# Identity matrices built on chip, a smaller load of constants, and a stored order in place of a planned one

## The chip, the cores and the metric

The kernel runs on one core of one Trainium2 chip. The metric is the time of one execution in microseconds of the device (us), the median of several executions. The engines are PE (TensorE, matmuls), DVE (VectorE), ACT (ScalarE), POOL (GpSimd) and SP (SyncE, which here only issues DMAs).

## What is computed

The inputs are q, k and v of shape (4, 8, 768, 64): 4 batches, 8 heads, 768 positions, 64 features. Attention is limited by a hash, and its result goes through a two-layer network:

```
q_bits = (q @ proj > 0); k_bits = (k @ proj > 0)        # proj is 64 x 6
mask   = bucket(q_bits) == bucket(k_bits)                # 6 bits make a bucket number
scores = where(mask, q @ k.T / 8, -1e9)
attn   = softmax(scores); x = (attn @ v) as (3072, 512)
h      = max(x @ w_in, 0)                                # w_in is 512 x 2048
out    = (h * h) @ w_out                                 # w_out is 2048 x 512
```

## The kernel before

**The work.** The program goes through 48 visits, one for each batch, third of the positions and pair of heads. A visit has four units of 128 queries (two heads, two blocks each). In a unit PE makes 128x768 scores in PSUM (`pS`, or `side`, or a bank of `po`), DVE takes the row maximum (tile `line`), ACT takes the exponential (tile `e`) with the row sums, and the reciprocal of the sums is `rv`. The masks need no work of their own: the keys and queries are extended by 64 rows that hold the codes of their buckets, so that one matmul adds a large negative number where the buckets differ.

**The preparation of a pair of heads** (`prep`) has these steps: the load of keys and queries (`A` and `Q` in the first batch, `R` later); the projection matmuls `pd`, which write `side` from `A`, `Q` and the projection `pj`; their signs `bits` by ACT; two matmuls per head with the code matrix `sgn` (`pc`, also in `side`); and DVE and ACT, which turn these into the extra rows. In the first batch, visits run "plain", in float32: the attention is transposed by PE against the identity `unit_f` (`pT`). Later visits use pairs of float16 numbers and transpose by DMA. The values V of a batch are scaled by their largest column norm, for which `dg` is made from a second identity, `ident` (`scale_values`).

**The network.** When the four pairs of heads of a third are done, its 256 rows go through both layers (`moe`): matmuls `pm` with `win`, ReLU and square, then matmuls `po` with `wo`. The weights are read, unpacked and split into two float16 parts during the first visits (`split_win`, `split_wout`, in the buffer `room`).

**The constants** (lines 806 to 833). `pj` (12 KB) and `cst` are loaded from ACT's DMA queue; `cst` is a tile of 128 rows whose first four columns are mask constants and whose other 128 columns are codes, of which rows 0 to 31 are used. `unit_f`, a 128x128 float32 identity, is loaded from SP's queue, and DVE copies it to `ident` in bfloat16 (line 832). In the planned program `cst` goes out ahead of `pj`. `bounded` (line 931) rescales two columns of `cst` by a factor tile `fac` once, before the first pair of heads that isn't plain.

**The order.** All operations are first written down in a list (`Program.add`) with the engines that may do each and the buffers they touch. `order` (line 509) then decides which engine does each operation, and in which order each engine has them, by a list scheduler (`forward`, `backward`) with a model of durations (`cost`, `LAGS`), shaken by about 1,500 stored seeds (`PATH`). The orders are fixed when the program is built: each engine takes its instructions strictly in turn, so one that waits holds back all behind it on its engine. In the model a small load from memory lands 2.2 us after its issue, whatever is queued in front of it (line 578). `emit` also puts matmuls of no use (`idle<-ones`) where the model sees PE idle before the first transposes.

Of the kernel before, what the change touches and what calls it, by code (L numbers as in the profile page):

```python
# [45 lines left out]
PRICE = dict(pe=1, dve=3.57, act=0.3, pool=3.06, sp=0.43)  # L46

EARLY, EARLY_TO = dict(pe=1, dve=1.5, act=1, pool=1, sp=0.43), 150000
AHEAD, DELAY, LAG = 60, 2500, 1.0

ROUNDS, BEHIND = 24, 40000
PATH = (
# [1253 lines left out]
```

## Time and profile before

| what | value |
|---|---|
| median of 3 executions | 869.58 us (869.0 to 869.71) |
| profiled execution: span from the first to the last instruction | 865.2 us |
| time around the span: median less span | 4.4 us |
| PE busy | 835.6 us (97%) |
| DVE busy | 660.7 us (76%) |
| ACT busy | 673.4 us (78%) |
| POOL busy | 73.7 us (9%) |
| HBM read | 37.36 MB |
| mean granted clock of TensorE | 0.994 of 2.4 GHz |

The page gives the profiled execution's span alone and no time around it; the 4.4 us are the median less that span. Busy shares are means over a span whose parts have different limits, so the stretches at the start are looked at by themselves below. A matmul in float32 leaves two records where one in float16 leaves one.

### The profile page before, as it was taken

What the parts mean: (1) busy time and instruction counts of PE and PEld (TensorE: products, weight loads), DVE (VectorE), ACT (ScalarE), POOL (GpSimd) and SP (SyncE); (2) the same over time, 40 slices, a digit from 0 to 9 for tenths busy, and PEclk for the clock granted to TensorE, in tenths of its full rate; (3) what the DMA queues carried; (4) which work ended last, traced back from release to release, by engine and by line L of the source; (5) the groups of instructions that cost most, each with busy time, mean ns of one, the idle gap of its engine ahead of it and who ended that gap; (6) DMA issues with size and microseconds to landing.
All of it is one profiled execution on the core that took longest, in us unless ns stands there. A gap on an engine that the chain in (4) does not pass through costs nothing. (4 is left out here: it accounts for less than half of the span.)

```text
span 865.2 us, 17070 instructions
## 1 busy us (share of the span) xinstructions
PE 835.6 (97%) x6386; PEld 548.4 (63%) x6386; DVE 660.7 (76%) x1450; ACT 673.4 (78%) x1185; POOL 73.7 (9%) x156
## 2 busy tenths in 40 slices
PE   6899899998999999999999999999999999999997
...
PEclk8999999999999999999999999999999999999999
...
GB/s 317 70 124 191 182 183 195 190 144 82 145 189 177 184 131 167 154 161 178 156 155 165 149 156 146 168 160 108 156 155 111 145 149 157 122 93 80 1 25 25
DMA packets 295361, 124.19 MB, mean 144 GB/s; under 512 B 273520, under 2 KB 281456, under 8 KB 295280
## 3 DMA queue, kind: packets, MB, share of 16 engines
...
HBM read 37.36 MB, written 6.29 MB: 50 GB/s over the span
## 5 line engine op out<-in xcount | busy, mean ns | idle before, releaser
L746 PE MATMUL pm<-xx,win 128*128 128x256 f16 x2304 | 308.7, 273 | 1.0 <-ACT g L746 0.7
L746 PE MATMUL po<-wo,g 128*128 128x512 f16 x1152 | 303.1, 379 | 5.1 <-ACT acc L746 2.9
L746 PEld LDWEIGHTS <-win 128*128 128x128 f16 x2304 | 223.4, 98 | 80.4 <-issue 12.8
L746 DVE SCALAR_TENSOR_TENSOR hl<-e,rv,hl 128x768 f16<-128x768 f32 x172 | 173.2, 1015 | 18.6 <-ACT hl L746 16.4
L746 PEld LDWEIGHTS <-g 128*128 128x128 f16 x1152 | 111.5, 98 | 104.5 <-issue 14.6
L746 ACT ACTIVATE hl<-e,rv 128x768 f16<-128x768 f32 x161 | 147.6, 928 | 8.6 <-DMA aT<-hl 7.5
L746 DVE SCALAR_TENSOR_TENSOR g<-g,g 128x512 f16<-128x512 f32 x90 | 61.8, 687 | 80.3 <-ACT g L746 80.0
L746 ACT ACTIVATE g<-g 128x512 f32<-128x512 f32 (+1 forms) x183 | 113.7, 626 | 8.9 <-PE po L746 6.5
L744 DVE TENSOR_REDUCE line<-pS 128x1 f32<-128x768 f32 x113 | 107.5, 952 | 14.1 <-PE pS L746 13.2
L746 ACT ACTIVATE g<-pm 128x512 f32<-128x512 f32 x94 | 55.5, 590 | 69.2 <-PE pm L746 66.7
L739 PE MATMUL pA<-aT,VV 128*64 128x256 f16 x1548 | 92.7, 274 | 0.0
L739 PEld LDWEIGHTS <-VV 128*64 128x64 f16 x1548 | 81.2, 110 | 14.2 <-issue 13.9
L746 ACT ACTIVATE e<-pS,pair 128x768 f32<-128x768 f32 x72 | 70.8, 984 | 17.8 <-DVE pair L744 12.6
L746 ACT ACTIVATE e<-side,pair 128x768 f32<-128x768 f32 x72 | 71.0, 987 | 14.6 <-DVE pair L744 9.7
L746 POOL TENSOR_SCALAR rv<-sm 128x1 f32<-128x1 f32 x104 | 32.7, 314 | 581.3 <-ACT e L746 579.4
L744 DVE TENSOR_REDUCE line<-side 128x1 f32<-128x768 f32 x79 | 75.2, 952 | 5.9 <-PE side L746 5.6
L746 ACT ACTIVATE e<-pS,line 128x768 f32<-128x768 f32 x41 | 36.8, 897 | 11.4 <-DVE line L744 10.1
L746 PEld LDWEIGHTS <-room 128*128 128x128 f16 x288 | 27.6, 98 | 19.0 <-issue 2.1
L746 PE MATMUL pS<-A,L 128*128 128x384 f32 x84 | 32.3, 494 | 2.2 <-ACT e L746 1.3
L746 PE MATMUL side<-room 128*128 128x384 f16 x144 | 34.3, 326 | 0.0
L746 PE MATMUL pS<-room 128*128 128x384 f16 x144 | 33.7, 326 | 0.4 <-ACT e L746 0.3
L746 PE MATMUL pS<-Q,M 128*128 128x384 f32 x80 | 32.2, 512 | 0.9 <-ACT e L746 0.6
...
## 6 DMA issues: line engine op xcount, KB each, us to landing
...
```

Of the source, the lines that this page charges most:

```text
L739: ins = q.engine.matmul(*map(real, args), **kw).ins
L744: issue(q, getattr(q.engine, name)(*map(real, args), **{k: real(x) for k, x in kw.items()}).ins)
L746: ins = getattr(q.engine, o.name)(*map(real, o.args), **{k: real(x) for k, x in o.kw.items()}).ins
```

## The change

The identities `unit_f` and `ident` are no longer loaded and copied: two `affine_select` instructions on POOL keep the diagonal of the tile of ones. Of the codes only rows 0 to 31 are loaded (16 KB in place of 66 KB). The mask constants become four memsets on POOL, at the size that `bounded` used to make with `fac`. The order in which the batch's first values are loaded is changed (`SPLITS`). The scheduler and its seeds are gone: a table packed into text (`ORDER`) holds the place of each operation and the engine that does it. The model stays only to place the idle matmuls; in it a small load now lands after 2.9 us (`LANDS`). The place where the idle matmuls stop is found as the first operation, in the new order, that uses their PSUM buffer.

```diff
+SPLITS = (1, 3, 0, 2)
...
-TRANSPOSES, HBM, SMALL = 165, 265, 300
+TRANSPOSES, HBM, SMALL, LANDS = 165, 265, 300, 2900
...
     def order(self):
         self.prepare()
-        out = self.rounds()
-        prio = None
-        for seed in PATH:
...
+        table = np.frombuffer(zlib.decompress(base64.b85decode("".join(ORDER.split()))), np.uint8).reshape(3, len(self.ops)).astype(int)
+        left = list(range(len(self.ops)))
+        out = [left.pop(n) for n in table[0] + 256 * table[1]]
+        for o, way in zip(self.ops, table[2]):
+            o.queue, o.name, o.args, o.kw = o.ways[way][:4]
+        self.replay(out)
         return out
...
                 if o.ways[0][4][1] < SMALL:
-                    dma, done = at0, busy + 2200
+                    dma, done = at0, busy + LANDS
...
-        for i in out[: out.index(self.busy_from)]:
+        busy = set().union(*(rec.ops for rec in self.idle[0].rec.line))
+        for i in out:
             o = self.ops[i]
+            if i in busy:
+                break
...
     act.dma_start(pj[:, 0 : 4 * NB], proj2[:, NB : 5 * NB])
-    both_f = sb([P, 4 + P], F32, "cst")
-    cst = both_f[:, 0:4]
-    act.dma_start(both_f, consts[:, 0 : 4 + P])
+    codes = sb([32, P], F32, "codes")
+    act.dma_start(codes, consts[0:32, 4 : 4 + P])
...
-        move(sgn[32 * n : 32 * n + 32, n * P : (n + 1) * P], both_f[0:32, 4:], 1.0, (dve, pool) if n else (dve,))
+        move(sgn[32 * n : 32 * n + 32, n * P : (n + 1) * P], codes, 1.0, (dve, pool) if n else (dve,))
...
-    unit_f = sb([P, P], F32, "unit_f")
-    sp.dma_start(unit_f, consts[:, 4 + 2 * P :])
-    ident = sb([P, P], BF16, "ident")
-    dve.tensor_copy(ident, unit_f)
+    unit_f, ident = sb([P, P], F32, "unit_f"), sb([P, P], BF16, "ident")
+    for x in (unit_f, ident):
+        pool.affine_select(x, ones, pattern=[[-1, P]], compare_op=ALU.is_equal, fill=0.0, base=0, channel_multiplier=1)
+    cst = sb([P, 2], F32, "cst")
+    for h, x, least in ((T, NB / 2 * MASK, -MASK), (U, (NB / 2 - 1) * MASK, 0.0)):
+        pool.memset(cst[h, 0:1], x)
+        pool.memset(cst[h, 1:2], least)
...
     def bounded(Rs):
         if not halved:
-            fac = sb([P, 1], F32, "fac")
-            for h, x in ((T, MASK / BIG), (U, MASK)):
-                dve.memset(fac[h], x)
-            dve.tensor_scalar(cst[:, 0:2], cst[:, 0:2], fac, 1.0, ALU.mult, ALU.mult)
...
-        for hp in range(H // 2) if b else START[1]:
+        for hp in range(H // 2) if b else SPLITS:
```

## Rows read from the trace of the kernel before

**Rows 1.** The page, 40 slices of 21.6 us: busy tenths, and PE's clock

```profile
PE   6899899998999999999999999999999999999997
PEclk8999999999999999999999999999999999999999
```

**Rows 2.** Busy us (instructions) by stretch: PE, weight load, DVE, ACT, POOL, clock, DMA

```profile
12.00:16.00 4.00, 0.78 (x3) 0.26 (x2) 0.03 (x1) 0.00 (x0) 0.00 (x0) 1.00 1.04 412
16.00:18.00 2.00, 0.30 (x1) 0.00 (x0) 1.94 (x4) 0.90 (x2) 0.00 (x0) 0.50 1.00 402
18.00:24.00 6.00, 6.00 (x23) 3.21 (x23) 4.27 (x10) 4.35 (x11) 2.86 (x4) 0.60 0.63 184
24.00:35.00 11.00, 8.70 (x50) 4.96 (x50) 10.33 (x29) 10.50 (x27) 1.15 (x2) 1.00 0.12 36
35.00:50.00 15.00, 13.53 (x84) 7.31 (x80) 13.51 (x27) 11.44 (x27) 2.92 (x7) 1.00 0.35 106
50.00:100.00 50.00, 45.42 (x274) 27.08 (x275) 45.96 (x103) 46.20 (x95) 18.75 (x31) 1.00 0.69 174
100.00:300.00 200.00, 194.64 (x1393) 124.44 (x1392) 173.81 (x378) 169.56 (x290) 26.81 (x45) 1.00 0.74 163
300.00:600.00 300.00, 297.56 (x2481) 199.72 (x2479) 245.85 (x542) 251.12 (x437) 12.77 (x42) 1.00 0.81 157
600.00:850.00 250.00, 248.59 (x1947) 167.98 (x1945) 157.44 (x340) 170.93 (x292) 7.67 (x20) 1.00 0.55 103
```

**Rows 3.** Timeline of the stall: start, us, engine, line, operation [idle before <-releaser]

```profile
8.92 0.33 SPq L746 DMA_DIRECT2D unit_f<-consts  x1
9.77 2.20 PE L746 MATMUL pS<-A,L 128*128 128x384 f32 x6 [0.94 <-ACT L L746]
...
15.97 0.23 DVE L746 CAST ident<-unit_f 128x128 bf16<-128x128 f32 x1 [6.35 <-DMA unit_f<-consts]
16.12 0.95 DVE L744 TENSOR_REDUCE line<-pS 128x1 f32<-128x768 f32 x1
...
18.14 1.54 PE L746 MATMUL pT<-unit_f,e 128*128 128x128 f32 x6
```

**Rows 4.** Waits in 0 to 35 us: who <- whom: us, times, longest

```profile
DVE ident L746 <- DMA unit_f<-consts: 6.3, 1, 6.3
...
ACT bits L746 <- PE pS L746: 1.5, 1, 1.5
...
DVE line L744 <- PE pS L746: 0.5, 1, 0.5
```

**Rows 5.** Timeline of the first loads and their users

```profile
0.73 0.41 ACTq L746 DMA_DIRECT2D cst<-consts  x1
...
1.17 0.46 ACTq L746 DMA_DIRECT2D pj<-proj  x1
1.19 0.42 SPq L746 DMA_DIRECT2D Q<-kq  x1
...
4.93 0.29 POOL L746 TENSOR_SCALAR sgn<-cst 32x128 bf16<-32x128 f32 x1 [3.91 <-DMA cst<-consts]
...
5.93 0.14 PEld L739 LDWEIGHTS side<-A,pj 128*32 128x32 f32 x3
```

**Rows 6.** Tiles `pj`, `Q` (0 to 20 us), `unit_f`, in turn: issue to landing

```profile
DMA to landing us min/median/max: 4.7/4.7/4.7
...
DMA to landing us min/median/max: 4.4/5.5/8.1
...
DMA to landing us min/median/max: 7.0/7.0/7.0
```

**Rows 7.** Groups of instructions on POOL: count | busy us, mean ns | idle before

```profile
L746 POOL TENSOR_TENSOR g<-g,g 128x512 f16<-128x512 f32 x6 | 7.6, 1260 | 33.9 <-ACT g L746 31.4 <-DVE g L746 2.4
...
L746 POOL TENSOR_SCALAR dg<-ident,top 128x128 bf16<-128x128 bf16 x1 | 0.4, 372 | 7.5 <-DVE top L746 7.5
```

**Rows 8.** Busy us in one stretch of 25 us

```profile
200.00:225.00 25.00, 22.39 (x178) 13.45 (x175) 20.01 (x46) 19.95 (x28) 0.19 (x1) 1.00 0.63 128
```

More of the change, by code (lines that the diff above doesn't have):

```diff
@@ L1 @@
-import heapq
-import random
+import base64
+import zlib
 from contextlib import ExitStack
@@ L45 @@
 BUFS = dict(xx=16, hl=3, e=3, aT=3, g=2, A=3, Q=3, L=3, M=3, RV=2, VV=6)
[L46 to L52, printed above, removed]
[194 rows of a table removed]
-)
+LAG = 1.0
+ORDER = """
+c-rlH2Vhji*8e#(x9x7WZ?f5JHY5-OBq5DR=*>pxT|`6>siBH=5KxK;$X}!=JVd2E0Z~8{1q2_8C{jd40>~o}nt)QJ!#8txH+%0UDEOhDzW+O6Z`-*uXU_c2IlnUt6(EYBj1m|vqDfXjY$b}K&~(s{
+4(1Mk(4PI_=FKp<*(4zB{sE9BR|g5~AYj|_@CXsw2!f%lC^`j_*0>swMzo0~nGjD!h&Dl)G$IjKX+aP~;`0(}ChRhDv?vI6A<C%;f+Xb#tfvU0jD|E2p|Y5l3_uBFBD96l6@=ChUkOT;L--^Pe7;zv
@@ new lines @@
+dwjCDRDr0JtqVSSvlcB=gEkNn9<JdLqL-ATWr5W7W=FOMPl5};l4`Ly!Qn8cO^C8XspN<VM??#6M3OBTY;Kz=&SZ+nF%gJ1Sd0dPp+c1>U4|zNk;cc%RkRvvwoNiXT0~``wA=x*vD6GD3DWO@#Ml({
+lF2c(v&z<tNs2*_r*bl_OQWOR_qf~D5ZqOx9!5whmE!`Z%jHT02h?jB1sV1@yVKs#Zma1@hIsbHeKwobnq8kAZB-%izBI5nvKyqBt2@jtu;xH2_5qTdMKZ-IAYlbxybohrW=LMIS7;0#8eKLz`XP_U
+BM9zNG}7a#?ukLy1FT!9Sh-dfW;-$*4&q9C$K|ry9f;OUYhvlFjD#e##APS=(qb*I`YOhF(-GV$QShFpK?M_(a~T25WhEjfnxrxy3M&{2L?ZMSgzJJ(P7s`eDscMJ>0f^OnNoU&(&Gv}dZG%GT!|k3
+85$fobqH%a3$nA1X48sXFe}TRnVFfNX~%RXjx>x)$j7bU`w*Nl<x*42?MV5k9Q>>H7D(D~akCK;%a)as-oY={FZ+0tEHA|+ON{abpKt9VpU*J=)cpBzanc)J?>m+0oH=ss*_CEh+Ea1Wd^%H@F=J;Y
@@ new lines @@
+OoJt4>eQ)=(r6AzO`QZOui=CV6R>>w)bi8Eu6%V&%5&3~v9%dBDr2O1;bij&bCTI?E?sWm$XNpijvB$P`<uB;HV-gIv$M-=hKTOH9j=}>=z>o|CxcaL+Y##4t&6SdRIO8|PU|{#8Ur?y<tFHnCEB<i
+b=MbZo%<eoAiEZ&4_430qM6m$?C;IwV*4Z$a?&c<($cII%4b%{sF0Bnm6e@sP08Y7EtN?!BFm?zv+vW=%xO@;>cS+m-5Qac%>E_YY-R99X<9llv2<B1edV4Dm#-Tykt<YbCNyn&x+#;NPs&ZWD2*F8
+{-tqaQqZVTBe~(8h7HRL_1)j)=ZZUbMbWK->+AbnTed~gFI-=`;}JGGVn2i2jk&p|Tqa=iIH}VKmMBY%<((^*8)<O$;@e9vxT{n-pIX_L<CoWRa*pQA&aqXhR0$$1d-ol1{M(Xgx4@pXTD5l8s#VKc
+vnJGl>V|4xLRBsslqyELmcKb9CnpBr^OdAxMfWFJ26(%3=2}YMLehyzhc};qj`&)K4mNZ+9H(cxXTD~gZne6mx~$d~Et*;LC)&ZbyD>Df+9Kfv>u3TKM;c(n_>9rQsEMPVeIAAylxGxWv@)PZ4XJwd
@@ new lines @@
+0VDh4h(Y~DsV@g;mACp=sWPl*_q;)*SLLpiJN4_{xpP<O`D9<A2XuP+3EGA9Z4X@@%gPgk$MF$F6oj@y3t5&O&5g~I*uAB>0U<ZHMXt}(q`r4W?t@+cc!+(VX02+qYu2#UAQ5)Ey)x5Lv}ReEqzV=$
+<;q(8Vm3#V@_{K9j4_f&bVs@UVs*PQDk@5jjFciJ7v(<eWOCIB(j@^d+Q>DA|I0q#4RSj6eC$uLzu-yXTnraDES)?moHz<cP8~Z@c=*Wa!opKWqR*Z<3{XH$5>hDdKkE2lpW~3jQQ+9U=j47z{sG5c
+$6;n%7QD9uY=c-~>(*UczZBrh%~Vn(=~LH6Hu?sq)3|m6Yv%aa;V`Z;n$2s>?{m*s#y-p0XDRm#C<WkKXmG>4IV>&UKaiPX#w?f#Cdh>8Mq}E`Mx&7!;f3or6K+go;ngtS@C!c~oTChepA3eR2E&hr
+i}G=L@)$i!jgsMz;oy~n5d{Y~9N18}YX9kog7;3r$^&ci^H;*ZfkOT}s{nSevED@s{u3c?Q{0z?EFxs_k`0R&Z&(|%e8t>(i+t}dUF!3#I8A1gISUCPhuLQu`@BisV8<zh%kwZ}CIY47rqXAhl~iG;
@@ new lines @@
+anjJqV}`P;XUC83CJpL3P?81?dw%42X#hMb_7layuk(l~_7|B7UGQmqs+%A@A&RkivFPQ}-s^4S^|n;6*+nz2w=cA*-<mCyC%2)ea~pR9to0B#RaL=Rr}2Xi)NRPty-rkA_4`?9?I~B50V;vz$&9Qu
+S(T1wt+r$bfU_UU&V%H#0LC&#<7}gnV2Cp$#3_nbiB%MIqlA$__-ff4)MAe@+w5k$$!K?gjSI0_(Rx$5af1@`HNJ@aaFsAbpE-jH3TK7W;u-uA(RR{yTz!LOMw_j`i3cPUL6CQWl)vlS?<D36vIILg
+aIV6o%a`HeSG%^rxy=Bl0e*t3r#8X~I0fgw5SV2P3ne&s&}b|;z(DW=uti@1?<zkitG?Z}>^+6ax0G&?7IF9aCv1c_mMpyri$7jGe+_>EtJ&uR8D=e9uwvoc3xI3=&zH<IAtEB;%{L+@vQxzDh%FKL
+0^+lDD*cp>nKnflIZm1)jgW@%)iezT;}8*`A4q)-L;DRGVCYK*C`0px%o;kxWa@4*nR=O2>1l%Y2v79t-7c?Vk7ro)=%y$glz=p4i`BCI<Kkm2+5yyW0ni#G5XHF-AN)sy*$R2^mHSmVvsN{*S}heE
@@ new lines @@
+%wSA1g{;)!X&GrlMy3vaMi?X{3+2_^*)Os0puv3y4io@HQc4iyuCm+%Jn%Rnd5;qoe;)19`EjJolUkEj@M!B!Pj>1Atw{6MgaEXaX~QNB8@Fso+dLvRYt^7-{U&0YN1BPPTl+_DDvI^QfK(Q%iPhDs
+x;eG)6*Fo8+zUYkQ-u^Esd7$|aPPfBd8DN&7vz2sOGp%>YocU{wK;4MZG%`#Y>dSN)Dh*2jqp;*W0hn@wy0i2MWocA207sOH?I@*%;h>EXU~#zYOmyHxN_z)$QNZ93@0vKI`-qmBNq<Axx$l$hkv<n
+;YVYE@nC`R*eOLJ1;?2&3r?IoaiSnT9|~B6IRvl^ASER=e@A)v9=?Wvd<kCoT)p}ngbj>cg5X&1SieRwn^#A`hism!&15wLA6t<3;%*9*nLj3GiSHsVJ_k21+*s`Manzn!0L%%`M4gDbbn)WRBgf81
+onu`d4GglEACCWceD5*Xb6^+OWzx<)dzcaj4jlM;2lHemOuro-_(p9%3}DmO8@CVH#vsj*yqSf`&j8lF$G&32F9*7E!zb@j`tI7drH_^`l>!3dGI7Dm_f~-L?p#55U05Q_7pzuc8cd%vXZj5Dv^S^P
@@ new lines @@
+rrKVy{bLS&kuB6z`ocdZPnk7)7JUgOGFVWMC&&yRqg8~B6^8j~nlMn{en=_w?7`e1Z}5<=J-V~>*L`S@!Gj0)>C?4aH>Q;glGNE?0FM$K4elr0?$&Pi!)`aT8p}g1U9Lv0b6d4;*wWR&)v&26v309f
+E>{cJgNFLd0c~|{xwcvss0~mJs^?UzVl-CHsm%J!f{GGkrn4)Oo|2*h0Payum7pHciyn+dj6!r_yxWPA-5!G?GHgbeObQx6ieQ0;#U@k|NCKejql_-H7YFgTFCbpx=RDQ+r~C_5cvOJH0zD`KH)xCf
+djOgUyO|Ys#pc$#r~5s-V!mZJH9N9HH9`1F;3Z2osYtTSO*0)ChAew}nxTR@^?tK#tD`E6AX0jrvLFx>qfj6h-~w@6hih!e)0d)+26fa3e)tLCIviH-YXR(oa|M@#y@!vSD%^YG5YT<n_jK28x<?HZ
+ut!n0vcG_A1^Hh*sBVzuwQ~OMO(@Y1Vc*^lu95d0>llAup(yVuCSo)$d3Tvnm4(Jd>Upj)D6_!u3XmCqpH0J;r{PpOWdKugvN%EP-8<qH(sKqGn?H_95}VOZOdbhs$}JwzYLpj-j~fv?Z(i&$=jd2<
@@ new lines @@
+O@<-%$AI)e?1f$XJ=L{OAH>c*M|ABs?5VDu`}FC~+d#h_0xSMHibEcw(Osk4^^a!qC_gmkhv>%a(<r)Wbc1@)4Vy$m1NZ%ILL(`y3s}3h%T=@LeKo3bhC^w!8g@HnnI?_><*;+6&1TN9TBS0QNs2d_
+k`(T|396;VhS8w17AC}I;5kjARoFTSgcXW1148;$@j6_BD~!8BV(IfxIzFDY_1R(pVxX)CV!;gwtS7!ug;vW?P+%%B{%D|VZ8>5Hb3)2O2rF=}?z{ZW&U}{QcDUe-A6;c(D{KOzv5>zE%(vHlzIoH8
+b@Hx!pkHqJX!Fjs8#amCz7kpVTXplAiuhH_$p*5_9}C}Q#{Vbchx0x_`#cL+-<oHhvyg*l7W=pCwWTwaEhd2JFS8)QJ$C)%kEcwV{qn3y%)$NM!xv=|j^%g<3xnP8Q7~q}z-JjDFv8$*PmdYYw?9{t
+$G|*+_UPHOzm(Tag5Dy3m#rFhP+wK$QD_D8n>T6Rs#(is%@#IauwcRLCbOHp+SCGO<22qt0WeGjrLIE9Q;Ak*Bxy9AFlxf{&(o1~6n*Z6i4!KMY7HjC1F^mzyY9`D>^*!$USdz^-MvT85k0&28&am*
@@ new lines @@
+;6Yq1=n+Rd(k{~DUM~xF<Vi+)A62PuGk#$4x9y`X8b1uVtwgbYbEmVOnA@^Nix#=cgY^}K^XOcwsip;LHEL{b(4Zz%tp_~e$W?fxNs}s8%t+5kuU4&E#=TY2vuoDOsaZn;NM?T-)GtiKQcSzj6}+i&
+sqt9a!U(zDV+XHIH3+LmtXB4k^~J`5g_<ZeQ_-oSL6RZ_JIjMsBND~r00-loUN0C02FfeI6lbqrynG$bBJmsdXMnT*t24(A{d@#?aa^^K1MDD(`^B`h0#;Fz@?`gS-{<F-`5qFI5_a9Q3sO>J++Ua7
+ndI|%++O$g=*Z}3cZ}P~Y@@~)8?ee8?2eCluqVu(KyGp*SP`!=W(6y+U%AW(8B4%~oF{J+a{4;p)vIq^Igclqd7bB+N8yC?Jk$0dz%jpm`vG>to_%n9?|$JZ9R9vgVj9ui^jivk$bHK}_a%c(WF*)(
++yAwF!}hIP*L}KW{l@j1xBh$E*7aX~Zr}8UWBZQvTemva+COxt-EIU}v%)`uxI~0^=|@XHTD|ClMU*aHNte=~z#Ky6a^B7yWA>t%bAsrcBflt2o%{OSxl@5oWGg_%%osoJ#c_ZW`%IiZZ7fWE?j=Uy
@@ new lines @@
+Cy<1Mgv8-PpCuCs1L61);|7i;<T*0De~^8UUZii}3c4|RM`;&I{a|Y!71b^(s%2CZA-vLR=yX0*AL`X}Jiy}1{r5TQuoJ0euTE_2qB8qr6ERE76f+=Qh6<2gAr<75tYj!(J`Kw8>`VE2CMFOP=l9e&
+Znr2jI%L_YOh$Bo2(m>UBLm^?C=nD`1K&*_s|v1M>+881)5~+&6La3vt;&Qh0Sp0*47w`}R6SdOg!1uw^GYSrIMsfn6d_d~gLVkcN=~;OvLe;SW;LZJfv7-fb3$4Il!17ND=V-LY#wVggHB{*%+2d8
+;{s1W*A$R1@C;<+hnxIxk{^D#D$AlI<{V;B+JB1hsC&}BhuC)U;^5#nHrqGf?DyJsGQY8Y%c={Dg?z@C-=~CkilXq@I;Jmt_yK&t=Kj8P;e(aJ@@?A$5SP=BfyzgZ$OM*>g^QUvmNSLt!#sdD*xy_j
+1*7J$xesSVYA8%oqb-YyFRDCcLO!J#R84wdD96)j3-%c|b_5J-pbTUK%TGN$^l1V5isG=RhxHlUdyv>md|Din*K5$|yg>s8vgbqLDd@`9K@__@L3+!bddhi&AMXf|N4m5p?OB?Ne3)|PjcmfrgciWU
@@ new lines @@
+Lc=EJMy<@|dg{iI`Tn|rv)Np|nz<IR6jX`Lx+3#PfXY-9?`3^g5XB^wX_u$*WjGUKEV-E)hunl1NTl+BDBDCL2nK;f$ONl^$TB~t;7lr{T)&Z$Tpq7V5@MMvoHCWdxD-tAVOc-jG(<+8Wcd?3PRIFk
+k?s@Rr6uDL$!eDjpomA615}nNy~aSY`_RFC1(yoW1+vIV{Pw_Z{NV>UvX8-Kd%+g?_l^L{zS{=y34Hw-?D|fIt&(A#!MM)2+W09m_6G)bw}KaN2E$Tr_P02bQONu6&nNIE&c}tYY)-_IdF+}IHk6IV
+*8yH)ZIqX}KLAXHnXgQmJ_&IQPDGqAea575Q%5tF;2q~3?wz1cYRs@8_ZWbE**l!N_Q+e?eNAsF(ysJ<AYE5<UA=nwlbt$1$EDzVti5m1s&=bZwp*~ARoBp_$XjMNdDS+3rjxS(fEg-uRQDMRbj*uW
+o}WB<j6g?EV77jS(#bDQdS)Vw$R0Xu+|c1enXcoXA2oLDV1NNEus<~-m0gVN!yVC<#0$x;YFB;wn7ViF`BcZJp6uJ#1VS%RDD6ZeAB$`o$>ib4$S#qsJGE}nu}x(2_K|*p)~-gbM;^(o_dsrwhoDg-
@@ new lines @@
+=Y3A7%OZ<d!!9-!tMW@GR(lrrGrOXsE6M4VE2ZCS^kdBoiIAx93OdnXh?OBGF;Pxrj>YEfie=2%&dPjysrWdH53CleN3j}BX7CsdZnr&(B}&=B>oaPxFrT+tMavELC;0ajSUid#SD2~KQqRTH9wRRS
+-0l;BeJS@b_rc(Gp?iP&o;_(5Dqs}ke~*}tjHT_A43@99?bs2st(0eb*=_E`#6-iEuMDi5iiz1A6SFDC3MO6zSUG<Y*+*gyVl>?Z`8uPc26}_BeI$l!mzZ;3T}IAd{^innDlC(vvp3J3xz6w}ii^%L
+H#+XGTMvp@cue5IO0XRL;phQFVWHW)tAH6O-+bu1Lj?ujo6Y;#6SJ9R=dWP<5Bq-jYA<ZfCts)p>I+~Das$BnH5)d3{MousKmB~orq9=|`E(5jK15ip8~^p*Cu^+hnZ|1YmI*6i-N$R!zO$Tu$Rnb>
+Og+x$2bC~Nv*)nSE1WvM`sTDZUw@sI!*j^A|M&XjDKC*1r_X+I606y4FvU9FYJCM?fl2u63&5(1aV%wwqI3wr2$lc_d-}(Y89VT~=LSX%U{>qL@C9MQmZu%1ZJ{;8VGACAoA~!=c<>DgVHG(uZbXD=
@@ new lines @@
+GVlN?DY9QAjWEzK8bNF}OYn6Ty1^`)%{To>V`E*V(s?*1if7K*&f09Jou`~mZv10#L{QaXHM(km-D-cT@YGY3c!6)LQ3!--f7QdX!eZquo^TeZbq|Z?JlxrDA&N~=Os0q!lc!|i!+~1-@iPmlfUNvi
+)wA&J7p|Y*c3v-(ENU|u+yVZ{1-PrShmN4gc0L6&H<Kx_5oa=MMJ@kiQ1@=t0oA=WCSbu}3(D4<X(!nHKb^2!PT>eM4RTw>#epwAKAx5+pwbI&+M+TbN{x|r)QE^2lHmW|Un-O!z}L*cmW5kC0Ajx>
+oKVCZ{N$e*hwqg@05X9+BbT6&;5_&j{>lQ;{}0u#?m#4via*5LcoE^QimEo1g7DBj{X<18ro`_PyrYR~gy>F1XZ<yYp!(;();{-t0xgLDTeT%4x`94Os5gQ|UF$Ut!jwNo6;FXy2z;wr{oy%$lG<B>
+D*OY(pxT-b#{8qGbzle;szrko8y5Y4{zLE{g9UWpeGDlbxWl5iv=hQ2HBqZ>P=UZx)HXrQKTT5%eGQ?Dz{C;4o@z~mx*M$l{t#CpCBlhlMk_LOF%anR0JoSGYEBsHI}nJ9kb)52E)=IUPiXLl=yby(
@@ new lines @@
+yo8pjNH5f{PM{eEL5xM<!O(!H$ANBk7#tEq%3{&z8VG@Q+!DZ~pY*SR;@3k7!vC2NeGJk(CpvT?68&U}#&?i}d=Z0drd^$oaWMo%5;zAvuBd&{ng>=iWK}Je5VW~a7cByKU;_vmz>rX+3xOisGjy>)
+AAi(=Scek&GpRm^>eSOrKjemT(OhKh*!uZ}M%0Bj9VTx-L*XBr#i2NR{@pJKcWD$sxLxyLNzPhAJTJBoMeD9}V0{=1;j0Lbpv4BDK7L{GV1U{vSUibf(PMoC(F9BVIGVH0TOn*h#XxhHP(w)ZU_(lb
+J1PecQXT($frt^%h!-M=`b;0PHimn&mO5Zjw$o2qXZfNGqg`6iETASc>2aYYH5wKaN?E};76L{wf5qZ?1t}nuTxk?fKza~qhhp^thU=#dI)Qm<GBbddi)rZq>f>XmnU3xi5xk&Q<X4x!WL^`fbwhlZ
+gmRak2!{${QpB7!yw{H)o~B3<1tc1ttRV~}JcR-1V=?N;C5BcGL$*ULe+)4h2&W=pOBQrY43Z<l>Ov4C?aO=)glA(V7&uTVF?c|@<A<gb;z$VE&;&XT7-UmAjD{GPE;eBCM5fE5#a&EKm%@V>ghLTR
@@ new lines @@
+9;q2w_Y7~9^@>-1zm;Hw|84FQK=^}GEr!LNVz3IgeHd>p7HKd<j>GvIfUbVh(Og{t2ATjEdZ590N$IY{z^2Q8I_h46Z|Q-l4NRb!hmPYT-a(oRufcV7ye3)sLs6&-C;C7YYUD521Ch-iiZm%6Lk^%#
+)FsXu^aT)NSa8zjLA`~k-Y&(wJUomPg^jSVr4I-?)}t$}z&~OUwbzuLVS5Dt;U#<tNi96b6{XgaDn8KWAYJ;_TBlg8iviMsA^M>mLX)X9iK?Xi91R01N@M}>1c5?8_iEq?32p@ic~PJXUfd9(^F*Rw
+@qi(TCN*OixRB@&qTS`t)K=P>E>z=Sr~=alY1K-+MpAz`m%?K^Z%>M4c(rp90!uh+0e$ugvEq=6187|(tm@a3XC0H%alDdqR~W~_FiYwQAL?=!BIsk0c4Gv>d_lvw;6F#gGKO~VEVPYX{1trwDn?~P
+<WiTfw7~}S8;-h=pv`Yk95ltVmp)BtYp$@Mg|{veF+2}y(WBE`yAy(_*=y503g2(T+d++{m?{>bNRUVum1-sJ0|hppISp0g7W(sDz>Y-Kju6muM1T@gi<U3wa|Y^dsNa_h<FndK1G?%@SALhcg@W25
@@ new lines @@
+2laYryV7n`hwao98|D_<dHVeZ{NHmw{8Kk}{wx1K3*OH6zgB+y%5CvLU-B;{7~K9TVIP46h(`$?@~c19gnt`wY7%NfLd8U}%?dv=!&^<LWG!wzd(aO{^kGB$gAM^Kxue^^#n5kqB_;|i3ih`E0|}a>
+s1fRxgWR2v6s{zqZsah<f|V8ALVFCT_G?hSO|?sCS2QM;0F>Vtmf-KR$6aWPn&LW~vW5SiSlr1<+;+iRrYh7RJp5PM@S>0CIwRq`+o31n>IN}_zx~7M@A&R7(GLHtak03$i~q>1hdqH?yn$g+?6*J`
+_J1YtmRKaeIS*3uT>m-<fxkN9e!Ifcw!&LjoZQj!+#;Ub)&O{CW04ZO#^0XNUFbSoYw~vtUGVn+Cj83c-XV_hHoCkUz5h|G^54*ecYjIY&U%Nt5n%p=XmQsuaF_Y+pNbXyooS2|PYCd*<QllkUBho@
+_rGfz`||+z2c)q(3}SbyIs74M>@Qz~{S_IuJ}=>&uF+i}GJokbcDKFzKY;Z9foUvk=k0Hj#_&HPjs5+%3GT4c|D9<J?=<WE7Xg1dk-@uMVB>#@%>P}x{{aV=9yt
@@ L248 @@
+"""
 LOADS = 0
@@ L331, in __init__ @@
         self.tc, self.ops, self.tags, self.n, self.rank = tc, [], {}, 0, 0.0
-        self.paced, self.marks, self.mark, self.busy_from = [], {}, None, 1 << 30
+        self.paced, self.marks, self.mark = [], {}, None
         self.first = []
@@ L467, in prepare @@
                 ops[j].users.append(i)
-    def rounds(self):
-        best, prio, ahead = None, [o.rank for o in self.ops], AHEAD
-        self.spans = []
-        for n in range(ROUNDS + 1):
-            out = self.forward(prio, ahead)
-            span = self.replay(out)
-            self.spans.append(span)
-            if best is None or span < best[0]:
-                best = span, out, self.state()
-            if n < ROUNDS:
-                prio, ahead = self.backward(), BEHIND
-        self.restore(best[2])
-        return best[1]
@@ L484, in draw @@
-    @staticmethod
-    def draw(seed, n):
-        x = np.arange(n, dtype=np.uint64) * np.uint64(0x9E3779B97F4A7C15) + np.uint64(seed * 0xBF58476D1CE4E5B9 & (1 << 64) - 1)
-        x = (x ^ (x >> np.uint64(30))) * np.uint64(0xBF58476D1CE4E5B9)
-        x = (x ^ (x >> np.uint64(27))) * np.uint64(0x94D049BB133111EB)
-        return ((x ^ (x >> np.uint64(31))) >> np.uint64(11)).astype(np.float64) * 2.0**-53
-    @staticmethod
-    def shake(prio, seed):
-        n = len(prio)
-        u = Program.draw(seed, n + 4)
-        kind, at, wide, by = u[:4].tolist()
-        noise = 2.0 * u[4:] - 1.0
-        if kind < 0.4:
-            lo, hi = float(prio.min()), float(prio.max())
-            near = np.abs(prio - (lo + at * (hi - lo))) < 10.0 ** (3.5 + 2.0 * wide)
-            return np.where(near, prio + 10.0 ** (2.0 + 2.0 * by) * noise, prio)
-        first = int(at * n)
-        last = first + int(10.0 ** (2.5 * wide)) + 1
-        step = np.zeros(n)
-        step[first:last] = noise[first:last] if kind < 0.7 else np.sign(noise[0])
-        return prio + 10.0 ** (2.3 + 2.2 * by) * step
@@ L509, in order @@
     def order(self):
         self.prepare()
-        out = self.rounds()
-        prio = None
-        for seed in PATH:
-            prio = np.array(self.backward()) if prio is None else prio
-            if seed:
-                prio = self.shake(prio, seed)
-                continue
-            self.replay(self.forward(prio.tolist(), BEHIND))
-            prio = None
-        if prio is not None:
-            out = self.forward(prio.tolist(), BEHIND)
-            self.spans.append(self.replay(out))
@@ L523, in order @@
-        return out
-    def state(self):
-        return [(o.queue, o.name, o.args, o.kw, o.start, o.busy, o.end) for o in self.ops]
-    def restore(self, kept):
-        for o, x in zip(self.ops, kept):
-            o.queue, o.name, o.args, o.kw, o.start, o.busy, o.end = x
+        table = np.frombuffer(zlib.decompress(base64.b85decode("".join(ORDER.split()))), np.uint8).reshape(3, len(self.ops)).astype(int)
+        left = list(range(len(self.ops)))
+        out = [left.pop(n) for n in table[0] + 256 * table[1]]
```

127 lines of the change are left out of this document (removed), and 194 rows, old and new, of the table PATH.

## The prediction

> **What bounds the kernel now.** I read the page's slices first. PE is at nine tenths or more in nearly all of them and lower in the first slices and the last one; its clock is below full in the first [rows 1]. So PE sets the time, and what can be won without taking matmuls away is PE's idle time and its time at the low clock. Second, the busy times by stretch say where that is [rows 2]. From 100 to 850 us PE is idle for 750 - (194.64 + 297.56 + 248.59) = 9.2 us, from 24 to 100 us for 76 - (8.70 + 13.53 + 45.42) = 8.35 us. In the 6 us from 12 to 18 it works for 1.08 us: the largest hole, and DVE, ACT and POOL are as empty until 16 us, while the DMA engines run at 412 GB/s. Third, the timeline of that hole [rows 3] and the waits [rows 4] name the cause. The first unit's scores are in PSUM by 11.97 us at the latest. DVE, which has to take their maximum, stands at the copy of `unit_f` to `ident`, 6.35 us idle, until the identity's load lands; the maximum starts at 16.12, behind the copy, on which it doesn't depend. The load took 7.0 us from issue [rows 6]: it was issued at 8.92 behind big loads. The planner had it at 2.2 us, a constant of its code, and so put the copy there. Fourth, the clock: it is still 1.00 in the hole, 0.50 (1.2 GHz) in the stretch behind it, 0.60 from 18 to 24 us, when PE is busy without a gap, and 1.00 again from 24 us [rows 2].
>
> From 24 us on DVE and ACT are the fuller engines at first (DVE 10.33 and ACT 10.50 of 11 us), then PE is; none of them waits for the first loads any more. A start that comes earlier by some us is therefore carried to the end, as long as the later order is as good.
>
> **The change part by part.**
>
> *The load of `unit_f` and its copy go.* The maximum, which started at 16.12, can start when the scores are there: 16.12 - 11.97 = 4.15 us earlier, less about 0.1 us for the hand-over, a gain of 4.0 us. Bounds: the six records of 9.77 to 11.97 hold one unit and a half (a float32 matmul leaves two, a unit has two matmuls), so the first unit could be complete after four of them, near 9.77 + 4 x 0.37 = 11.25, which would give 4.9; and if another late wait takes this one's place, the gain is nothing. I take 4.0, the value that the rows bear without a guess. Next late would be the transposes, which need `unit_f` on PE: 18.14 - 4.0 = 14.1 us. The 64 KB taken from the DMA engines are 0.16 us at 412 GB/s, and SP's queue is 0.33 us shorter; nothing waits for either by the rows, so I take 0.
>
> *Two selects on POOL.* No row of before has one. The nearest rows are an operation of POOL on the same 128x128 elements, 0.37 us, and as the dear end a two-input one on 128x512, 1.26 us [rows 7]; below, a copy of 32x128 took 0.29 [rows 5]. Two cost 0.74 us, by the bounds 0.6 to 2.5. POOL stood idle for 3.91 us up to 4.93 [rows 5], which hides any of these. Queued behind the selects on POOL are a copy of codes into `sgn` and later work; if the cover went, that copy would wait, and it can as well be put on DVE. For the transposes the selects have until 14.1 us. Taken: 0, bounds 0 to 0.5 us lost. The four memsets that make `cst` anew are of the same kind, and the first users of `cst` come only in the second batch: 0, with the same bounds. The three small DVE instructions on `fac` and `cst` that go stood ahead of a projection's copy, not ahead of anything that was late: 0, up to 0.3 us gained.
>
> *Clock.* From 18 to 24 us PE was busy for 6.00 us at 0.60, work of 3.6 us at full clock: at most 2.4 us lost. DVE and ACT were busy for 4.27 and 4.35 us of these 6, so not all was PE's. The waits that name PE here are 1.5 us of ACT (`bits`) and 0.5 of DVE (`line`) [rows 4]. Without the hole the clock should hold. I take 1.0 us, half of these waits, with bounds 0 and 2.4.
>
> *Projections first, 32 rows of codes.* PE's first real work, the projections, began at 5.93. `pj` was issued second on ACT's queue, at 1.17, and took 4.7 us: 5.87. `Q` was issued at 1.19 and landed at the soonest 4.4 us later, at 5.59 [rows 5, 6]. With `pj` first, `Q` sets the start: 0.3 us gained. The codes come second, so at 1.17 + 4.7 = 5.87 if they take as long as `pj` did; the four copies into `sgn` then end about 0.9 us later, by 6.8, and the signs that they are multiplied with were ready about 7.45. Bounds: 0.5 lost (if the codes are later by that much) to 0.5 gained. The rule of the Trainium skill that bears on loads speaks against all of this part: the page "DMA: Bandwidth & Descriptors", section "Anatomy of one DMA", gives one transfer about 2.0 us and its bytes at 436 GB/s. By it the estimate for the identity's 64 KB is 2.15 us, the load would have landed before the scores were there, and the sum without the 4.0 us would be 1.3. The row has 7.0 us, with other loads in the queue; it decides, and I keep 4.0.
>
> *The order anew.* This touches every instruction behind the start. What the new table holds can't be read from the profile. Bounds: at best it takes away much of the 17.5 us of PE's idle time between 24 and 850 us, half of it being 8.8; at worst it adds as much, which is as far from the rows of before as from a perfect order. I take 0. The new number for small loads, 2.9 us, is still under the 4.0 to 4.7 of the trace for `cst` and `pj`, but there are only two such loads left, both at the very start. The idle matmuls stay where the model sees PE idle: 0, bounds 0.5 either way.
>
> Sum: 4.0 + 1.0 + 0.3 = 5.3 us. The profiled span goes from 865.2 to 859.9. With the 4.4 us between the span and the median of the runs, 869.58 becomes 864.3 us.
>
> **The rivals.**
>
> *The hole is filled by something else.* DVE and ACT are at 94 to 95% from 24 to 35 us and 92% from 50 to 100 [rows 2], so work that came earlier might be followed by a longer wait, for the third pair's loads above all: loads issued in the crowded stretch took up to 8.1 us [rows 6]. Against it: those loads are used much later than they land, and DMA is nearly quiet from 24 to 35 us (36 GB/s). Then only the clock and the start remain, or part of the stall: 0 to 1.7 us, 868 to 869.6. A case of the same time is that the selects end after 14.1 us, on which each us late costs one; by the prices above they would need five times the dearest row.
>
> *The new order is worse in the body.* The place is the stretch of 100 to 300 us, where PE has the most idle time in the body, 5.4 us, and where one stretch of 25 us alone lost 2.6 [rows 8]. The mechanism: preparations of later pairs of heads sit in DVE's and ACT's queues in a fixed turn; if the new order puts the masks of a pair behind other work, PE's matmuls on them wait and everything behind them with it. Each such stretch costs 2.6 us. The gain of 5.3 and the margin of 1.7 are used up from three more such stretches on (7.8 us): 872.1, slower than before. For it: the old planner's mistake on a load shows that a wait which the model misjudges stands in the final order. Against it: no slice behind the first ones shows a hole like theirs [rows 1].
>
> *The new order is better in the body.* If it takes away a third of the 17.5 us, 5.8, the time is 858.5. For it: PE's many short waits are what an order can change. Against it: PE is at 97 to 99% from 100 us on.
>
> **How the numbers follow.** A measurement of this kernel can tell 0.2%, 1.74 us, from no change: the same is 867.8 to 871.3. I give the forecast 0.61 (860 to 867.8), the better order 0.13 (under 860), the refilled hole 0.12 (the same), and the worse order 0.14 (over 871.3). So faster is 0.61 + 0.13 = 0.74, same 0.12, slower 0.14. The range for 8 in 10 goes from 858.5 to 871.0: it leaves out about 0.06 below, where more than a third of the body's idle time goes, and the worse order above.
>
> **What would show it.** In the new profile no DVE instruction waits for a load of `unit_f`; the first maximum starts near 12 us and the first transposes near 14; PE's clock stays at 1.00 from 12 to 24 us; the projections start near 5.6 us; the selects end well before 14 us. PE's idle time from 24 to 850 us should be near 17.5 us: if it is far from that, the order is what decided, and the forecast is right or wrong by another cause than mine. I am wrong if the early stages lead by 5 us and the end doesn't, or if DVE stands at a new load near 12 us.

## The result, and the profile after

The changed kernel takes 857.16 us (855.65 to 857.55) against 869.29 us (866.66 to 869.71) before: a ratio of 0.9856, 95% interval 0.9835 to 0.9876, or 12.1 us less where 5.3 were forecast, and under the low end of 858.5. The profiled span went from 865.2 to 855.8 us, 9.4 us less. The two differ because the profiled execution of before was a short one: the spans of eleven others were 865.8 to 867.5 us (of 23 more, 863.6 to 867.7), with a time around them of 2.1 us. So about half of the 4.4 us that the forecast took for the time around the span was spread.

The stretches of the changed kernel, in the columns of [rows 2]:

```profile
12.00:16.00 4.00, 3.70 (x21) 1.51 (x19) 3.74 (x7) 3.27 (x6) 0.19 (x1) 1.00 1.04 404
16.00:18.00 2.00, 1.51 (x5) 0.92 (x6) 1.80 (x4) 2.00 (x6) 0.25 (x1) 1.00 1.04 404
18.00:24.00 6.00, 3.94 (x22) 2.65 (x22) 5.81 (x14) 5.17 (x14) 1.25 (x4) 0.96 0.65 252
24.00:35.00 11.00, 10.77 (x63) 5.73 (x61) 8.60 (x21) 9.14 (x22) 3.14 (x5) 0.87 0.01 1
35.00:50.00 15.00, 13.42 (x85) 7.70 (x83) 13.94 (x31) 12.81 (x27) 5.54 (x9) 1.00 0.54 148
50.00:100.00 50.00, 47.77 (x301) 28.82 (x298) 45.98 (x99) 45.91 (x95) 17.54 (x26) 1.00 0.67 174
100.00:300.00 200.00, 197.90 (x1425) 126.74 (x1423) 170.64 (x381) 170.23 (x297) 46.65 (x59) 1.00 0.76 167
300.00:600.00 300.00, 297.06 (x2460) 199.81 (x2459) 243.52 (x550) 249.19 (x433) 14.73 (x37) 1.00 0.80 153
600.00:850.00 250.00, 247.91 (x1932) 166.49 (x1930) 151.10 (x316) 167.87 (x284) 8.89 (x23) 1.00 0.54 103
```

The reader should see three things. The hole is gone: PE works for 5.21 us of the six from 12 to 18, where it worked for 1.08. The clock is better but not full: 0.96 and 0.87 in two stretches. And PE's idle time from 24 to 850 us is 826 - 814.83 = 11.2 us instead of 17.5: 2.1 us less in 24 to 35, 2.4 in 50 to 100 and 3.3 in 100 to 300, and 1.2 more in 300 to 850. The removed load has little part in the stretches from 50 us on: with the old order and no load (experiment 1) PE's idle time from 50 to 850 us is 13.1 us, against 13.8 before and 9.4 now.

The start of the changed kernel, as in [rows 3] and [rows 5]:

```profile
1.12 0.29 POOL L430 TENSOR_SCALAR_AFFINE_SELECT unit_f<-ones 128x128 f32<-128x128 bf16 x1
1.37 0.29 POOL L430 TENSOR_SCALAR_AFFINE_SELECT ident<-ones 128x128 bf16<-128x128 bf16 x1
...
6.07 0.14 PEld L423 LDWEIGHTS side<-A,pj 128*32 128x32 f32 x2 [0.20 <-DVE L L430]
...
11.66 0.96 DVE L428 TENSOR_REDUCE line<-pS 128x1 f32<-128x768 f32 x1 [1.74 <-PE pS L430]
...
13.70 0.77 PE L430 MATMUL pT<-unit_f,e 128*128 128x128 f32 x5
```

The selects take 0.29 us each and end by 1.7 us. The first maximum comes at 11.66 instead of 16.12 and the transposes at 13.70 instead of 18.14. The projections start no earlier (6.07 against 5.93).

### The profile page after: what moved, and what is told of

It is laid out like the page before. It is cut to its first block, busy times and chain, and to the rows that moved or that the text cites. A ratio compares the mean times of both kernels' runs of the same rounds, so it can differ in the third digit from the quotient of the medians.

```text
span 855.8 us, 17059 instructions
## 1 busy us (share of the span) xinstructions
PE 835.2 (98%) x6386; PEld 548.4 (64%) x6386; DVE 651.5 (76%) x1434; ACT 670.3 (78%) x1183; POOL 99.9 (12%) x176
## 5 line engine op out<-in xcount | busy, mean ns | idle before, releaser
L430 ACT ACTIVATE hl<-e,rv 128x768 f16<-128x768 f32 x166 | 152.7, 929 | 6.8 <-DMA aT<-hl 3.0
L430 ACT ACTIVATE g<-g 128x512 f16<-128x512 f32 (+1 forms) x183 | 113.9, 626 | 13.4 <-PE po L430 10.9
L430 DVE SCALAR_TENSOR_TENSOR g<-g,g 128x512 f16<-128x512 f32 x84 | 57.5, 687 | 74.9 <-ACT g L430 74.5
L430 POOL TENSOR_SCALAR rv<-sm 128x1 f32<-128x1 f32 x98 | 35.4, 361 | 544.7 <-ACT e L430 544.4
L423 PEld LDWEIGHTS <-VV 128*64 128x64 f16 x1548 | 81.3, 110 | 15.2 <-issue 13.1
L430 ACT ACTIVATE e<-side,pair 128x768 f32<-128x768 f32 x72 | 71.1, 987 | 11.3 <-DVE pair L428 8.2
```

The source lines that it names most:

```text
L423: ins = q.engine.matmul(*map(real, args), **kw).ins
L430: ins = getattr(q.engine, o.name)(*map(real, o.args), **{k: real(x) for k, x in o.kw.items()}).ins
```

## Experiments

Each was timed beside runs of the kernel before; their medians in the four sets were 868.97, 868.0, 868.75 and 867.96 us. These differ by 1 us, so a difference of two kernels from different sets is no better than that. An order is a list of operations with an engine for each. Since nearly all operations of the two programs are the same, one program can be given the order of the other, or part of each. The old and the new order differ in the turns, and in the engine of 211 of the 7,253 operations.

**1. All of the change but the order.**

```diff
 the changed program
-ORDER = the new table
+ORDER = the old order, with the selects and memsets behind POOL's memset of ones_f
-SPLITS = (1, 3, 0, 2)
+SPLITS = (1, 2, 3, 0)
```

> The changed program with every engine's old order: identities by POOL's selects, 32 rows of codes, constants by memsets, the codes still ahead of the projection, the old order of the value loads. Theory A (the hole at 12 to 18 us is worth 4.4 to 5 us, the rest is the new order's): 863 to 865 us, 6 to 8 us above the changed kernel. Theory B (the late identity put the whole old order out of step, and without it the old order is as good as the new): 856 to 859 us. In both the first row maximum starts near 11.7 us.

862.66 us, ratio 0.9932 (0.9919 to 0.9944). Theory A: the load and the small edits are worth 6.3 us, and 5.5 to 6 us are left for the order (4.9 to 6.6 if each kernel is set against the runs of before beside it). Theory B is out. The first maximum came at 10.95 us, not near 11.7. The clock does not explain the order's part: the executions with a mean granted clock of 1.000 have spans of 858.7 and 860.7 us here and of 853.9 to 855.1 in the changed kernel's two sets. Of the 5.5 us some 0.7 lie around the span (2.4 us here, 1.7 in the changed kernel), and no row says why.

**2. The load back in the new order.**

```diff
-    for x in (unit_f, ident):
-        pool.affine_select(x, ones, ...)
+    sp.dma_start(unit_f, consts[:, 4 + 2 * P :])    # behind the third load of Q
+    dve.tensor_copy(ident, unit_f)                  # ahead of the first row maximum
```

> The changed kernel in its new order, but the identity is loaded from memory behind the third load of Q and copied on DVE ahead of the first row maximum, as before. Theory A: the hole returns, 4.5 us of it, and a spell at the low clock: 861 to 863 us. Theory B: the whole loss returns: 867 to 870 us. A third possibility, that the new order hides the load: within 1 us of the changed kernel.

864.31 us, 0.9953 (0.9941 to 0.9965): 7.2 us over the changed kernel, between the ranges of A and B. In its timeline DVE stands at the copy again:

```profile
9.11 0.33 SPq L426 DMA_DIRECT2D unit_f<-consts  x1
...
16.54 0.23 DVE L426 CAST ident<-unit_f 128x128 bf16<-128x128 f32 x1 [7.28 <-DMA unit_f<-consts]
16.68 0.95 DVE L424 TENSOR_REDUCE line<-pS 128x1 f32<-128x768 f32 x1
```

The load costs about the same under either order, 6.3 us (with the small edits) and 7.2, and the order gains about the same with the load, 868.97 - 864.31 = 4.7 us (again with the small edits), as without it, 5.5. The two parts add up.

**3. to 5. Where the order's gain lies: three cuts, new first.**

```diff
-ORDER = the new table
+ORDER = the first 428 (1183, 2144) operations of the new order, the rest in the old
```

> The changed program in the new order for its first 428 operations (up to about 60 us in the plan), then in the old order. Theory A with the gain of the order behind 60 us (between 85 and 250 us, where the new trace gains 4 to 5 us on the old): as the whole old order, 863 to 865 us. If the order's gain lies in the first 60 us: 857 to 859 us.

> The changed program in the new order for its first 1183 operations (up to about 150 us in the plan), then in the old order. With the cut at 60 us it took 861.61 us. If the order's gain between 85 and 120 us is the 1.8 us that the two traces show, 859.5 to 860.5 us; the rest, up to the changed kernel's time, then lies behind 150 us. If all of the gain is behind 150 us: 861.5 to 862.5 us. If all is ahead of it: 857 to 858 us.

> The new order for the first 2144 operations (up to about 260 us in the plan), then the old. With the cut at 150 us it took 860.06 us. If the gain of the order behind 150 us is that of the stretch at 160 to 230 us, where PE is idle for 2.7 us less: 856.5 to 858 us. If it is spread over the rest of the run: 859 to 860.5 us.

861.61 us (0.9902 to 0.9926), 860.06 us (0.9893 to 0.9924) and 856.74 us (0.9846 to 0.9876). From the old order's 862.66 the steps are 1.05 us up to 60 us, 1.55 to 150, 3.3 between 150 and 260, and nothing behind; as ratios to the runs beside them they are 1.6, 0.5 and 4.1 us. Only the third step is larger than the intervals; the first two are argued from the traces. PE's busy time in three stretches (the columns are those of [rows 2]) shows idle times of 3.89, 4.72 and 4.31 us in the old order:

```profile
60.00:150.00 90.00, 86.11 (x560) 55.08 (x565) 81.88 (x169) 79.60 (x150) 30.50 (x45) 1.00 0.79 195
150.00:260.00 110.00, 105.28 (x764) 65.46 (x762) 97.07 (x222) 95.19 (x155) 5.62 (x14) 1.00 0.72 144
260.00:840.00 580.00, 575.69 (x4641) 386.58 (x4640) 427.45 (x937) 445.50 (x770) 21.85 (x66) 1.00 0.70 136
```

2.06, 5.06 and 4.15 us with the new order up to 150 us:

```profile
60.00:150.00 90.00, 87.94 (x577) 56.41 (x577) 83.27 (x174) 82.19 (x158) 35.38 (x45) 1.00 0.77 190
150.00:260.00 110.00, 104.94 (x762) 65.13 (x761) 97.00 (x222) 93.36 (x152) 6.32 (x14) 1.00 0.72 148
260.00:840.00 580.00, 575.85 (x4643) 386.92 (x4642) 427.56 (x937) 446.17 (x770) 22.18 (x66) 1.00 0.70 136
```

and 2.13, 1.86 and 5.03 us in the changed kernel:

```profile
60.00:150.00 90.00, 87.87 (x576) 56.32 (x576) 82.91 (x174) 81.69 (x158) 34.82 (x45) 1.00 0.78 189
150.00:260.00 110.00, 108.14 (x797) 67.62 (x797) 92.04 (x213) 91.23 (x154) 23.35 (x27) 1.00 0.74 158
260.00:840.00 580.00, 574.97 (x4634) 386.05 (x4629) 425.67 (x937) 446.75 (x768) 25.90 (x66) 1.00 0.70 134
```

PE's idle time falls just in the stretch that has the new order, by 1.8 us and by 2.9; behind 260 us it is 0.7 more. (The stretches hold not quite the same work, as the runs lead by some us.)

**6. The other cut, old first.** The first 436 operations in the old order, the rest in the new.

> The changed program in the old order for its first 436 operations (up to about 60 us in the plan), then in the new order. Theory A with the gain of the order behind 60 us: 857 to 859 us, as the changed kernel. If the order's gain lies in the first 60 us: 863 to 865 us.

858.48 us (0.9858 to 0.989): most of the gain is behind 60 us, as expected.

**7. and 8. What the order does at 150 to 260 us: engines.** There the second weights are rescaled, by 16 operations of 128x1024. The old order has all on ACT, the new one 11 on POOL.

```diff
-new order: 11 rescalings on POOL, 5 on ACT
+new order: 16 on ACT
-old order: 16 rescalings on ACT
+old order: 11 on POOL, 5 on ACT
```

> The changed kernel in its new order, but all 16 rescalings of the second weights (128x1024, about 1.14 us each) are on ACT, as in the old order, instead of 11 on POOL and 5 on ACT. Theory A1 (a good part of the order's gain of about 5 us is that these 12.5 us of work leave ACT between 180 and 210 us, where PE then waits less): 859 to 861 us, with PE idle about 2 to 3 us more in 175 to 215 us. Rival A2 (the sequence of the masks and matmuls there, not the engine): within 1 us of the changed kernel.

> The changed program in the old order (862.66 us), with the same 11 of the 16 rescalings of the second weights moved from ACT to POOL, and nothing else. A1: 859.5 to 861 us, PE's waits between 185 and 215 us gone or halved. A2: 862 to 863.5 us, the waits of PE for the extra rows L stay at about 2 us.

866.81 us (0.9971 to 0.9998) and 865.92 us (0.9957 to 0.9984): each order gets worse with the other's engines, by 10 and by 3.3 us. Neither theory gave either time: A1 had 859 to 861 us for the new order and 859.5 to 861 for the old one, A2 at most 1 us over the times without the move. In the new order PE then waits for ACT's work, which has the rescalings ahead of it:

```profile
PE pc L426 <- ACT bits L426: 2.9, 1, 2.9
PE po L426 <- ACT wo L426: 2.3, 1, 2.3
PE pc L426 <- ACT M L426: 1.8, 1, 1.8
PE pA L419 <- ACT M L426: 1.8, 1, 1.8
```

So moving some operations to another engine in a fixed order says little about why the order is better.

**9. and 10. The rescalings' work taken out of both orders.** Most of the rescaling is left out here; its instructions and their turns stay.

```diff
-            x = wo[:, :, n]
+            x = wo[:, :, n, 0:2]
```

> The changed program in the old order (862.66 us), with each of the 16 rescalings of the second weights done on 128x4 numbers instead of 128x1024: most of that work is left out, the instructions and their turns stay. Theory S1 (the old order loses behind 150 us because ACT has 18 us of rescalings in its queue there): about 859 to 860 us, and within 1.5 us of the changed kernel less its own rescalings and the 2.6 us that the orders differ by ahead of 150 us; PE's waits for L near 205 us gone. Theory S2 (the sequence of the masks, not the rescalings): 861.5 to 862.7 us, PE's waits for L stay.

> The changed kernel (856.7 to 857.2 us) with the same rescalings cut to 128x4 numbers. S1: 855.5 to 856.7 us, since 11 of them are on POOL, which has room; the two small waits for the masks at 183 to 190 us may go (1.2 us). S2: the same.

863.54 us (0.9925 to 0.9954) and 855.93 us (0.9848 to 0.9882). Without 16 x 0.85 us of work on ACT the old order gains nothing, so that work is not what it loses by: S1 is out (the time is a little over S2's range too). What is left is the rest of the order, its turns and its other engines, which no run parts from each other. DVE's turns in the run with the old order show a place:

```profile
205.29 0.66 DVE L427 TENSOR_SCALAR L<-pc,cst 128x384 f16<-128x384 f32 x1
205.87 0.23 DVE L427 TENSOR_SCALAR both<-both 128x2 uint32<-128x2 uint32 x2
206.01 0.61 DVE L427 TENSOR_SCALAR hl<-e,rv 128x768 f16<-128x768 f32 x1
206.53 0.35 DVE L427 TENSOR_SCALAR own<-both 64x2 f32<-64x2 f32 x2
206.92 1.02 DVE L427 SCALAR_TENSOR_TENSOR hl<-e,rv,hl 128x768 f16<-128x768 f32 x1
207.86 0.16 DVE L427 TENSOR_SCALAR both<-both 128x4 uint32<-128x4 uint32 x1
207.93 0.67 DVE L427 TENSOR_SCALAR L<-pc,cst 128x384 f16<-128x384 f32 x1
```

and PE's turns beside them:

```profile
206.01 0.32 PE L427 MATMUL pc<-bits,sgn 128*128 128x384 bf16 x1 [0.48 <-DVE L L427]
206.17 1.24 PE L427 MATMUL po<-wo,g 128*128 128x512 f16 x5
208.65 0.32 PE L427 MATMUL pc<-bits,sgn 128*128 128x384 bf16 x1 [1.24 <-DVE L L427]
```

The second code matmul `pc` starts at 208.65, when DVE has made the mask `L` (207.93 to 208.60), and DVE makes it in its turn, behind the two steps `hl` that split the attention, of 0.61 and 1.02 us. The matmuls behind `pc` wait with it. In the old order with its full rescalings (experiment 1) the same waits stand, with the same sizes (from 178 to 222 us):

```profile
PE pc L427 <- DVE L L427: 2.0, 3, 1.2
PE po L427 <- DVE acc L427: 0.8, 1, 0.8
PE pd L420 <- DMA R<-kq: 0.4, 1, 0.4
PE pm L427 <- DVE g L427: 0.3, 1, 0.3
```

In the changed kernel PE doesn't wait for DVE in this part (170 to 215 us):

```profile
PE pc L430 <- ACT L L430: 0.8, 1, 0.8
PE pc L430 <- ACT bits L430: 0.5, 1, 0.5
PE pS L430 <- ACT e L430: 0.2, 1, 0.2
PE pm L430 <- ACT g L430: 0.2, 1, 0.2
```

Over the whole of 150 to 260 us the waits of PE add up to 4.6 us in the old order, 3.3 of them for `L` and `acc` (the network's sums) from DVE, and to 1.9 us in the changed kernel, none of them for DVE. That is 2.7 of the 2.9 us. It is read from two traces; no run moved these masks alone.

**11. All 16 rescalings on POOL, in the new order.**

> The changed kernel with all 16 rescalings on POOL, the 5 of ACT too (5.7 us of work). If ACT is the engine that PE waits for there: 855 to 856.5 us. If the order fits its own choice of engines, as the move of all of them to ACT showed (866.81 us): 858 to 862 us, PE's second matmuls waiting for POOL.

863.25 us (0.9929 to 0.9954), 6 us worse and over both ranges: the second matmuls wait for POOL once, for 4.6 us. All on ACT and all on POOL are both worse than the new order's 11 and 5; numbers between were not tried.

**12. The clock behind the hole.** Experiment 2 with 54 more idle matmuls in the hole (`fill[39] = 54`).

> The new order with the identity loaded and copied as before (864.31 us without this edit), and 54 more idle matmuls on PE in the hole, ahead of the matmul that waited 5.9 us there, to keep PE busy and its clock up. If the low clock behind the hole (6.8 us at half in that trace) costs 1 us, as forecast: 863 to 863.5 us. If it costs 2.4 us or more: 861 to 862 us. If the cost is all the wait itself: 864 to 865 us. The hole itself stays in each case: the maximum starts near 16.7 us.

865.51 us (0.9954 to 0.9978), over all three ranges, and inconclusive. The idle matmuls took 3.2 us, and the low clock came all the same, for 3.4 us instead of 6.8 (0.72 in 18 to 24 us); but the identity landed 1.2 us later in that execution, and the first maximum started at 17.91.

**13. Fewer idle matmuls ahead of the projections** (`fill[26] = 36`, 46 before).

> The changed kernel with 36 instead of 46 idle matmuls ahead of the first projections. If these hold the projections back (they end at about 6.1 us, when keys, queries and the projection have landed), the projections start near 5.4 us and the time is 0.3 to 0.7 us less, 856 to 857 us. If a load sets the start: projections at 5.9 to 6.1 us and no change.

859.93 us (0.9869 to 0.9906): no gain, and its interval reaches that of the changed kernel. The projections did start earlier, at 5.21 us, so the idle matmuls held them back. But DVE's queue then had:

```profile
7.95 0.56 DVE L431 TENSOR_SCALAR M<-Q 64x768 f32<-64x768 f32 x1 [1.73 <-DMA Q<-kq]
8.51 1.01 DVE L431 TENSOR_SCALAR A<-side 64x384 f32<-64x384 f32 x2
...
12.27 0.96 DVE L429 TENSOR_REDUCE line<-pS 128x1 f32<-128x768 f32 x1 [2.15 <-PE pS L431]
```

The masks `A`, ready earlier, stood behind a copy that waited for the second load of Q, so the scores began 0.2 us later than in the changed kernel (10.26 against 10.07). The first maximum came 0.6 us later. The rest goes with the clock: PE had been idle from 8.1 to 10.26 us, the clock fell to half behind that, at about 11.3, and the first six records of the scores took 3.25 us instead of 2.20. The first line is of the timeline, the second is the stretch of 12 to 16 us in the columns of [rows 2], with a clock of 0.67:

```profile
10.26 3.25 PE L431 MATMUL pS<-A,L 128*128 128x384 f32 x6 [2.18 <-ACT L L431]
12.00:16.00 4.00, 3.88 (x13) 2.12 (x12) 3.06 (x5) 1.81 (x4) 0.19 (x1) 0.67 1.03 407
```

This is one execution. Two of the five had a mean clock of 1.000 and took 856.56 and 857.65 us, about the changed kernel's time; the other three, at 0.995 to 0.997, took 859.93 to 860.94.

**14. The changed kernel again.**

> The changed kernel again, beside the others on the same chip: 856.5 to 858 us by every theory; its spread shows which of the differences can be told apart.

856.71 us (855.62 to 859.43), 0.9876 (0.9857 to 0.9894). No version was faster than it beyond the intervals; the one with 2144 operations of the new order equals it.

## Why the prediction was wrong

**The failed step** is "*The order anew* ... I take 0." It is worth 862.66 - 857.16 = 5.5 us, or 5.9 against the second set of the changed kernel, and with the 6.3 us of the rest it makes up about the 12.1. The bounds (8.8 us either way) held it, and the rival of a better order named 5.8 us and 858.5; but I gave it 0.13. I had the right rows and didn't follow them: PE was idle for 17.5 us in the body, [rows 8] was in the worst part of it, and the waits from 100 to 300 us named DVE's masks and sums, which stand in DVE's queue at the turn that the order gives them:

```profile
PE pc L746 <- DVE L L746: 2.0, 3, 1.2
PE po L746 <- DVE acc L746: 1.3, 2, 0.8
```

The new order is without both. I weighed it as a coin with equal sides. Where its gain lies is shown for 150 to 260 us only; the part ahead of that is within the intervals, and what turns and engines do apart stays open.

**The hole** was right in mechanism and near in size, 4.0 taken. The first maximum comes 1.6 us behind the start of the first scores in the changed kernel (10.07 and 11.66) and in experiment 1 (9.35 and 10.95), so before, where the scores began at 9.77, it could have come at 11.36 instead of 16.12: 4.8 us, inside the bound of 4.9. The changed kernel gained 4.46 by this sign because its scores began 0.3 us later, and experiment 1 gained 5.2 because they began 0.4 earlier. **The clock**, taken at 1.0, is not shown by itself. With the load gone from the old order everything came to 6.3 us; beside the 4.8 of the hole and the 0.4 of the earlier start 1.1 are left for it and all else, inside the bounds 0 to 2.4. The experiment meant to price it by itself failed. The clock does not hold from 12 to 24 us as I wrote: it is 0.96 in 18 to 24.

**Projections first** was wrong in mechanism: neither `pj` nor `Q` sets the start in the changed kernel; the idle matmuls ahead of them do (with ten fewer the projections began at 5.21 us instead of 6.07). Nor does the turn of `pj` matter: in experiment 1, with the codes issued ahead of it, they began at 5.53. The 0.3 us did not come, and starting them earlier did not help. **The selects** were right (0.29 us each, hidden). **The rule** of the Trainium skill on a transfer's time ("DMA: Bandwidth & Descriptors", section "Anatomy of one DMA — SWDGE (gpsimd) path") is given there for transfers that GpSimd issues. This load was issued by SP, behind others, and took 7.4 us from issue to DVE's copy in the second experiment, as against the 2.15 of that estimate; no run shows the load with nothing in front of it. **The rivals** of a refilled hole and of a worse body are out: the lead is kept, and PE's idle time in 100 to 300 us fell from 5.4 to 2.1 us.

**The time around the span** was a slip of method: I took the median of some executions less the span of another. It did no harm to the forecast, since taking it off and putting it back on leaves 869.58 - 5.3, but the 859.9 that I gave for the span was set on a short execution: with 2.1 us around it the profiled execution took an estimated 867.3 us.
